# A 2x2 block product with seven products in the second matmul of a retention-plus-MLP kernel

## Chip, cores, metric

One core of a Trainium2 chip. The metric is device time in microseconds (us) of one execution. The kernel before takes 217.24 us (median of 4 runs, 216.81 to 218.08). Ratios and their intervals are those over fast runs, so they are not quite the ratio of the medians that are quoted. A run counts as slow when it is over 1.5% above the fastest of the same kernel in the same call.

## The reference

Causal linear attention with a decay per head, then an MLP with tanh-GELU. Four sequences of 768 tokens, 8 heads of 64, so 3072 tokens of width 512; the MLP is 512 to 2048 to 512.

```python
for t in range(S):
    state = gamma[None, :, None, None] * state + np.einsum('bhd,bhe->bhde', k[:, :, t], v[:, :, t])
    y[:, :, t] = scale * np.einsum('bhd,bhde->bhe', q[:, :, t], state)
# x: y as (3072, 512)
h = x @ w_in
g = 0.5 * h * (1.0 + np.tanh(c * (h + 0.044715 * h * h * h)))
out = g @ w_out
```

## The kernel before

The sequence is cut into 6 chunks of 128 positions; a chunk has 4 x 128 = 512 rows. "M1" of a chunk is `x @ w_in` with GELU, "M2" is `g @ w_out`. While TensorE works on M1 and M2 of chunk c, the attention of chunk n = c + 1 is woven in: GpSimd scales and casts its inputs (`prep`), VectorE transposes them (`att_T`) and evicts masked scores, that is, moves them from PSUM, where matmuls write, to SBUF (`att_AY`); TensorE does the small products.

```python
# GpSimd: scale q, transposed k, k; cast v   (once per chunk and sequence)
def prep(c, b):
    for nm in "qk":
        if c in BLK[nm]:
            prep_blk(nm, c, b)          # tensor_tensor, two SBUF inputs (fp32), fp16 out
    prep1(nc.gpsimd, "k", c, b)         # tensor_tensor, two SBUF inputs
    prep1(nc.gpsimd, "v", c, b)         # cast, one SBUF input
# pool of the scaled transposed k: bufs=2; freed by VectorE's transposes

# M2: 64 matmuls of 512 columns a chunk
def moe2_mm(ps, c, b, fcs, n0, n1):
    for fc in fcs:
        nc.tensor.matmul(out=ps[:, n0:n1],
            lhsT=g_sb[c, fc // 2][:, fc % 2, b * C:(b + 1) * C],
            rhs=w_out_sb[fc // (NF // NO)][:, fc % (NF // NO), n0:n1],
            start=(fc == 0), stop=(fc == NF - 1))

# the weaving, chunks 2 to 4; the key is the unit after which the work is issued:
# units 0 to 15 are M1 (0.86 us each), 16 to 31 are M2
after = {
    2: [(prep, n, 0)], 4: [(prep, n, 1)],
    6: [(prep, n, 2), (att_T, n, 0)], 8: [(prep, n, 3), (att_T, n, 1)],
    9: [(load, n + 1)] if n + 1 < NCk else [],
    12: [(att_AY, n, (), "att", n, (0, 1), None)],      # first scores
    13: [(att_T, n, 2)], 15: [(att_T, n, 3)],
    18: [(att_AY, n, (0, 1), "h", n, (2, 3), VE)],      # second scores
    # ... state sums after 20, 21, 27, 28
}
```

Of the kernel before, what the change touches and what calls it, by code (L numbers as in the profile page):

```python
# [9 lines left out]
F16 = mybir.dt.float16  # L10
F32 = mybir.dt.float32
AF = mybir.ActivationFunctionType
ALU = mybir.AluOpType
# [3 lines left out]
def kernel(  # L17
# [9 lines left out]
    nc = tc.nc  # L27
    B, H, S, Dh = q.shape
    C = 128
    NCk = S // C  # L30
    NHP = H // 2
    n_tok, d_model = out.shape
    d_ff = moe_w_in.shape[1]
    NF = d_ff // 128
# [23 lines left out]
    const = ctx.enter_context(tc.tile_pool(name="const", bufs=1))  # L58
    ld = ctx.enter_context(tc.tile_pool(name="ld", bufs=2 * B))
    pre = ctx.enter_context(tc.tile_pool(name="pre", bufs=2 * B))  # L60
    att = ctx.enter_context(tc.tile_pool(name="att", bufs=4))
    xp = ctx.enter_context(tc.tile_pool(name="xp", bufs=2))
    gp = ctx.enter_context(tc.tile_pool(name="gp", bufs=2))
    op = ctx.enter_context(tc.tile_pool(name="op", bufs=4))
    psum = ctx.enter_context(tc.tile_pool(name="psum", bufs=1, space=bass.MemoryType.PSUM))

    OQ, OK, OG, OT = 0, H, 2 * H, 2 * H + NHP
# [58 lines left out]
    def hold(nm, c, b, until):  # L126
# [19 lines left out]
        out=misc[:, 0:1], in_=zero[:, 0:1], func=AF.Gelu_apprx_tanh, scale=1.0  # L146
# [16 lines left out]
    for j in range(2):  # L163
        for hp in range(NHP):
            nc.vector.tensor_scalar(
                out=mask[:, j, hp],
                in0=cst[:, OT:OT + 128],
# [64 lines left out]
    def bank(tag, dt=F32, shape=(128, NHP, 128), name="ps"):  # L232
        return psum.tile(list(shape), dt, tag=tag, bufs=BANKS[tag], name=name)
# [156 lines left out]
    w_out_sb = [const.tile([128, NF // NO, d_model], F16, name=f"w_out{i}") for i in range(NO)]  # L390
# [16 lines left out]
    g_sb = {}  # L407

    def moe1_mm(c, fc, out, t0, t1):
        wi, wr = w_in_of[fc]  # L410
        for kc in range(NHP):
            nc.tensor.matmul(  # L412
                out=out,
                lhsT=w_in_sb[wi][:, kc, wr * 128:(wr + 1) * 128],
                rhs=xT[c][:, kc, t0:t1],
                start=(kc == 0),
                stop=(kc == NHP - 1),
                skip_group_check=True,
            )

    def g_tile(c, fc):
        if (c, fc // 2) not in g_sb:
            g_sb[c, fc // 2] = gp.tile([128, 2, B * C], F16, tag=f"g{fc // 2}", name="g")
        return g_sb[c, fc // 2]

    def gelu(out, in_):
        nc.scalar.activation(out=out, in_=in_, func=AF.Gelu_apprx_tanh, scale=1.0)  # L427

    def moe1(c, fc):
        h_ps = bank("h", shape=(128, B * C), name="h_ps")  # L430
        moe1_mm(c, fc, h_ps, 0, B * C)
        gelu(g_tile(c, fc)[:, fc % 2], h_ps)

    def moe1_two(c, fp, t0, t1):

        h_ps = bank("h", shape=(128, 2, B * C // 2), name="h_ps")
        for r in range(2):
            moe1_mm(c, 2 * fp + r, h_ps[:, r, 0:t1 - t0], t0, t1)
        gelu(g_tile(c, 2 * fp)[:, :, t0:t1], h_ps[:, :, 0:t1 - t0])

    o_ps = {}

    def moe2_mm(ps, c, b, fcs, n0, n1):
        for fc in fcs:
            nc.tensor.matmul(  # L445
                out=ps[:, n0:n1],
                lhsT=g_sb[c, fc // 2][:, fc % 2, b * C:(b + 1) * C],
                rhs=w_out_sb[fc // (NF // NO)][:, fc % (NF // NO), n0:n1],
                start=(fc == 0),
                stop=(fc == NF - 1),  # L450
            )

    def moe2(c, b, fcs, tag="o"):
        if fcs[0] == 0:
            o_ps[c, b] = bank(tag, shape=(128, d_model), name="o_ps")
        moe2_mm(o_ps[c, b], c, b, fcs, 0, d_model)

    def ev_O(c, b):
        ps = o_ps[c, b]
        rows = out[b * S + c * C:b * S + (c + 1) * C, :]  # L460
        o_sb = op.tile([128, d_model], F32, tag="o", name="o_sb")
        if b == B - 1 and c > 0:
            nc.vector.tensor_copy(out=o_sb, in_=ps)
        else:
            nc.scalar.copy(out=o_sb, in_=ps)  # L465
        if c == NCk - 1:
            eng = nc.scalar
        else:
            eng = nc.sync if c == 0 and b < B - 1 else nc.gpsimd
        eng.dma_start(out=rows, in_=o_sb)  # L470

    def moe2_last(c, b):

        hw = d_model // 2
        rows = out[b * S + c * C:b * S + (c + 1) * C, :]
        o_sb = op.tile([128, d_model], F32, tag="o", name="o_sb")
        for i in range(2):
            ps = bank("h", shape=(128, d_model), name="o_ps")
            m0, m1, m2 = i * hw, i * hw + hw // 2, (i + 1) * hw
            moe2_mm(ps, c, b, range(NF), m0, m2)  # L480
            if i == 0:
                nc.vector.tensor_copy(out=o_sb[:, m0:m2], in_=ps[:, m0:m2])  # L482
            else:
                nc.vector.tensor_copy(out=o_sb[:, m0:m1], in_=ps[:, m0:m1])
                nc.scalar.copy(out=o_sb[:, m1:m2], in_=ps[:, m1:m2])
            nc.sync.dma_start(out=rows[:, m0:m2], in_=o_sb[:, m0:m2])

    def run(units, after):
        for i, u in enumerate(units):
            u()  # L490
            for f, *args in after.get(i, ()):
                f(*args)

    VE, AC, PO, SY = nc.vector, nc.scalar, nc.gpsimd, nc.sync
# [88 lines left out]
    def units2(c, b, n=4, tag="o"):  # L583
        u = [(lambda i=i: moe2(c, b, range(i, i + n), tag)) for i in range(0, NF, n)]
        last = u[-1]
        u[-1] = lambda: (last(), ev_O(c, b))
        return u


    def preps(c, b):  # L590
# [15 lines left out]
    run(  # L606
        [u[i % 3][i // 3] for i in range(12)] + u[3],
        {
            8: [(preps, 1, 0)],
            10: [(att_T, 1, 0), (preps, 1, 1)],  # L610
            11: [(att_AY, 1, (), "att", 1, (0,), None)],
# [9 lines left out]
    for b in range(B):  # L621
# [5 lines left out]
            for fp in range(NF // 2)  # L627
        ],
        {
            1: [(att_AY, 1, (2,), "o", 1, (3,), VE)],  # L630
            3: [(att_S, 1, 2)],
            4: [(att_AY, 1, (3,), "o", 1, (), VE)],
            6: [(att_S, 1, 3)],
            8: [(att_T, 2, 0), (load, 3)],
            10: [(att_T, 2, 1)],
            12: [(att_AY, 1, (), "o", 2, (0, 1), None)],
            14: [(att_T, 2, 2)],
            15: [(att_T, 2, 3)],
        },
    )  # L640
    run(
        [x for b in range(B) for x in units2(1, b)],
        {
            2: [(att_AY, 2, (0, 1), "h", 2, (2, 3), AC)],
            4: [(att_S, 2, 0)],
# [5 lines left out]
    )  # L651


    for c in range(2, NCk - 1):
        n = c + 1
        after = {
            2: [(prep, n, 0)],
            4: [(prep, n, 1)],
            6: [(prep, n, 2), (att_T, n, 0)],
            8: [(prep, n, 3), (att_T, n, 1)],  # L660
            9: [(load, n + 1)] if n + 1 < NCk else [],
            12: [(att_AY, n, (), "att", n, (0, 1), None)],
            13: [(att_T, n, 2)],
            15: [(att_T, n, 3)],
            18: [(att_AY, n, (0, 1), "h", n, (2, 3), VE)],
            20: [(att_S, n, 0)],
            21: [(att_S, n, 1)],
            25: [(att_AY, n, (2, 3), "h", n, (), AC)],
            27: [(att_S, n, 2)],
            28: [(att_S, n, 3)],  # L670
        }
        run(
            [(lambda fc=fc: moe1(c, fc)) for fc in range(NF)]
            + [x for b in range(B) for x in units2(c, b)],
            after,
        )
    c = NCk - 1
    for fc in range(NF):
        moe1(c, fc)
    for b in range(B - 1):  # L680
        for x in units2(c, b):
            x()
    moe2_last(c, B - 1)


# [28 lines left out]
```

## Time and profile before

| | before |
|---|---|
| time | 217.24 us |
| TensorE busy | 207.2 us, 96% of the span |
| M2, a chunk | 64 matmuls of 512 columns, 13.8 us |
| GpSimd's preparations in M1 of a steady chunk | 16, back to back, 14.3 us |
| VectorE busy | 82.9 us, 38% |

TensorE bounds the kernel; the prediction shows the lines. The groups by shape (line, engine, operation, output from inputs, shapes, count, then busy us and mean ns of one, then idle time before) give what VectorE and GpSimd do over the whole run:

```profile
L278 DVE TENSOR_TENSOR a_sb<-a_ps,mask 128x512 f16<-128x512 f32 x48 | 30.2, 684 | 19.6 <-PE a_ps L265 19.5
L188 POOL TENSOR_TENSOR k<-k,cst 128x512 f16<-128x512 f32 x24 | 25.1, 1047 | 16.4 <-DMA k<-in_k_dram 16.4
...
L199 POOL TENSOR_TENSOR q<-q,cst 128x512 f16<-128x512 f32 x16 | 16.7, 1042 | 5.8 <-DMA q<-in_q_dram 5.8
```

GpSimd's products take two tensors from SBUF, 1.04 us each. VectorE's big group takes one from PSUM and one from SBUF.

### The profile page before, as it was taken

How to read it: one execution, taken by the hardware profiler on the slowest of the kernel's cores; microseconds unless marked ns; L12 is line 12 of the kernel's file. 1: busy time of each engine (PE TensorE's matmuls, PEld its weight loads, DVE VectorE, ACT ScalarE, POOL GpSimd, SP SyncE). 2: the span in 40 equal slices, each digit the busy share in tenths (PEclk: the TensorE clock that was granted, in tenths of full speed). 3: DMA queues.
4: the chain of work that ended last, by engine and by line, in shares of the span. 5: the costliest groups of instructions: out<-in, count | busy, mean ns of one | idle time of the engine just before them, and what ended most of it. 6: DMA issues, size and time to landing. Idle time of an engine off the chain costs nothing.

```text
span 215.8 us, 3912 instructions
## 1 busy us (share of the span) xinstructions
PE 207.2 (96%) x1544; PEld 112.9 (52%) x1544; DVE 82.9 (38%) x152; ACT 87.0 (40%) x150; POOL 96.9 (45%) x116
## 2 busy tenths in 40 slices
PE   7889999999979999999999999999999999999993
PEld 2447644457867655444545444545444545444462
DVE  3445200198635562153691343682344650100001
ACT  2585562254444233276223275223366123476120
POOL 3699200324169542699433799412399321100000
PEclk9999999999999999999999999999999999999999
DMA  7999999896899688998679977579910012100111
GB/s 172 288 249 207 206 205 240 201 319 129 176 242 190 107 156 160 267 266 125 104 140 241 264 140 117 80 153 252 260 37 3 0 49 87 62 0 0 52 75 71
DMA packets 124417, 32.88 MB, mean 152 GB/s; under 512 B 118064, under 2 KB 122544, under 8 KB 124400
## 3 DMA queue, kind: packets, MB, share of 16 engines
q1 hardware_dynamic: 107984, 20.58, 48.2%
q0 software_dynamic: 5584, 8.65, 17.0%
q10 hardware_dynamic: 10832, 3.41, 6.5%
q8 instruction: 12, 0.20, 0.4%
q14 instruction: 5, 0.04, 0.1%
HBM read 30.53 MB, written 6.29 MB: 171 GB/s over the span
## 4 chain that ended last, share of the span: by engine, by line
PE 83%; SPq 4%; DMA 4%; POOL 2%; ACT 2%; issue 1%; DVE 1%; ACTq 0%; POOLq 0%; DVEq 0%
PE o_ps L445 38%; PE h_ps L412 34%; SPq L114 4%; PE a_ps L265 3%; PE y_ps L300 3%; DMA iden<-rr_ident 2%; PE s_ps L319 2%; DMA q<-in_q_dram 2%; PE y_ps L287 2%; PE qkT_ps L242 1%; PE spin_ps L152 1%; POOL q L199 1%; POOL k L188 1%; ACT qkT L224 1%; ACT g L427 1%
## 5 line engine op out<-in xcount | busy, mean ns | idle before, releaser
L445 PE MATMUL o_ps<-w_out,g 128*128 128x512 f16 (+1 forms) x400 | 88.1, 371 | 0.0
L412 PE MATMUL h_ps<-xT,w_in 128*128 128x512 f16 (+2 forms) x488 | 86.6, 334 | 0.5 <-ACT g L427 0.5
L427 ACT ACTIVATE g<-h_ps 128x512 f16<-128x512 f32 (+1 forms) x98 | 57.4, 588 | 51.6 <-PE h_ps L412 51.6
L412 PEld LDWEIGHTS <-w_in 128*128 128x128 f16 x488 | 45.8, 98 | 36.9 <-issue 0.7
L445 PEld LDWEIGHTS <-g 128*128 128x128 f16 x400 | 37.7, 98 | 38.8
L278 DVE TENSOR_TENSOR a_sb<-a_ps,mask 128x512 f16<-128x512 f32 x48 | 30.2, 684 | 19.6 <-PE a_ps L265 19.5
L188 POOL TENSOR_TENSOR k<-k,cst 128x512 f16<-128x512 f32 x24 | 25.1, 1047 | 16.4 <-DMA k<-in_k_dram 16.4
L470 POOL DMA_DIRECT2D out_dram<-o_sb x17 | 9.7, 568 | 46.4 <-ACT o_sb L465 36.8
L465 ACT COPY o_sb<-o_ps 128x512 f32<-128x512 f32 x19 | 11.0, 585 | 42.3 <-PE o_ps L445 37.1
L345 POOL TENSOR_TENSOR stg<-st,cst 128x512 f32<-128x512 f16 x16 | 16.4, 1045 | 10.2 <-DVE st L336 9.1
L336 DVE TENSOR_TENSOR st<-s_ps,stg 64x256 f16<-64x256 f32 x32 | 13.5, 421 | 17.8 <-PE s_ps L319 17.2
L199 POOL TENSOR_TENSOR q<-q,cst 128x512 f16<-128x512 f32 x16 | 16.7, 1042 | 5.8 <-DMA q<-in_q_dram 5.8
L251 DVE STREAM_TRANSPOSE qkT<-q 128x512 f16<-128x512 f16 x16 | 11.2, 700 | 13.1 <-POOL q L199 13.1
L224 ACT CAST xT<-y_ps 128x512 f16<-128x512 f32 x15 | 8.3, 588 | 12.2 <-PE y_ps L300 12.1
L199 POOL TENSOR_TENSOR kT<-kT,cst 128x512 f16<-128x512 f32 x12 | 12.5, 1042 | 0.0
L188 DVE TENSOR_TENSOR q<-q,cst 128x512 f16<-128x512 f32 x7 | 4.8, 686 | 19.0 <-DMA q<-in_q_dram 18.9
L152 PE MATMUL spin_ps<-zero 128*128 128x512 f16 x32 | 9.9, 449 | 1.2 <-DVE zero L144 1.2
L482 DVE COPY o_sb<-o_ps 128x256 f32<-128x256 f32 x1 | 0.4, 424 | 25.2 <-PE o_ps L445 25.2
L185 POOL CAST v<-v 128x512 f16<-128x512 f32 x16 | 9.6, 601 | 0.0
L183 ACT CAST v<-v 128x512 f16<-128x512 f32 x8 | 5.0, 622 | 11.1 <-issue 7.9
L251 DVE STREAM_TRANSPOSE qkT<-kT 128x512 f16<-128x512 f16 x12 | 8.3, 690 | 1.7 <-POOL kT L199 1.7
L226 DVE CAST xT<-y_ps 128x512 f16<-128x512 f32 x9 | 5.9, 687 | 7.8 <-PE y_ps L300 7.8
(33 smaller groups left out, 96.9 us busy)
## 6 DMA issues: line engine op xcount, KB each, us to landing
k<-in_k_dram SPq DMA_DIRECT2D x22, 256.0 KB, 4.4
v<-in_v_dram SPq DMA_DIRECT2D x18, 256.0 KB, 4.4
out_dram<-o_sb POOLq DMA_DIRECT2D x17, 256.0 KB, 3.5
q<-in_q_dram SPq DMA_DIRECT2D x64, 64.0 KB, 2.6
kT<-in_k_dram SPq DMA_DIRECT2D x48, 64.0 KB, 2.7
w_in<-in_moe_w_in_dram POOLq DMA_DIRECT2D x4, 512.0 KB, 9.6
w_out<-in_moe_w_out_dram POOLq DMA_DIRECT2D x4, 512.0 KB, 15.0
v<-in_v_dram ACTq DMA_DIRECT2D x6, 256.0 KB, 5.5
```

Source lines behind the costliest of these rows:

```text
L152: nc.tensor.matmul(out=ps, lhsT=zero[:, 0:128], rhs=zero, start=True, stop=True)
L188: eng.tensor_tensor(out=t, in0=src, in1=cst[:, col:col + H].unsqueeze(2).broadcast_to([128, H, Dh]), op=ALU.mult,)
L199: nc.gpsimd.tensor_tensor(out=t, in0=ld_all((key, c))[:, b * NHP:(b + 1) * NHP].rearrange("p hp a d -> p (hp a) d"), in1=cst[:, col:col + ...
L224: eng.copy(out=out, in_=in_)
L251: nc.vector.transpose(out=t[:, i].rearrange("p hp t -> p (hp t)"), in_=blk16.pop((nm, c, b)).rearrange("p ha d -> p (ha d)"),)
L278: nc.vector.tensor_tensor(out=s, in0=ps[j], in1=mask[:, j], op=ALU.mult)
L336: eng.tensor_tensor(out=st[sl, :, b, sl], in0=s_ps[sl, :, sl], in1=stg[sl, :, b, sl], op=ALU.add,)
L345: nc.gpsimd.tensor_tensor(out=stg[:, :, b], in0=st[:, :, b], in1=cst[:, OG:OG + NHP].unsqueeze(2).broadcast_to([128, NHP, 128]), op=ALU.mult,)
L412: nc.tensor.matmul(out=out, lhsT=w_in_sb[wi][:, kc, wr * 128:(wr + 1) * 128], rhs=xT[c][:, kc, t0:t1], start=(kc == 0), stop=(kc == NHP - ...
L427: nc.scalar.activation(out=out, in_=in_, func=AF.Gelu_apprx_tanh, scale=1.0)
L445: nc.tensor.matmul(out=ps[:, n0:n1], lhsT=g_sb[c, fc // 2][:, fc % 2, b * C:(b + 1) * C], rhs=w_out_sb[fc // (NF // NO)][:, fc % (NF // NO ...
L465: nc.scalar.copy(out=o_sb, in_=ps)
```

## The change

The intent: M2 of a chunk is a 2x2 block product (rows in halves by sequence parity, the inner dimension in halves by parity of the 128-blocks, columns in halves). The block form with seven products needs 7/8 of the matmul columns. Price: four sums of 512 elements for every four GELU blocks, 16 a chunk (VectorE, fp16, both inputs in SBUF), 16 sums of weight blocks once, and PSUM banks that ScalarE copies out in the middle of an accumulation ("snapshots"). Its core:

```diff
+    def g_sums(c, i, p0=0, p1=2):
+        ...
+        tt(t[1], q[0, 1], q[1, 1], ALU.add)          # tt: nc.vector.tensor_tensor
+        tt(t[3], q[0, 0], q[0, 1], ALU.subtract)
+        tt(t[2], t[1], q[0, 0], ALU.subtract)
+        tt(t[4], q[1, 0], t[2], ALU.subtract)
+    PROD = (                      # bank, left, right, opens, closes
+        ("X", (0, 0), (0, 0), True, False),
+        ("Z", 1, 1, True, False),
+        ("X", 2, 2, False, False),
+        ("Z", 4, (1, 1), False, True),
+        ("X", 3, 3, False, False),
+        ("Z", (1, 0), (1, 0), True, True),
+        ("X", (1, 1), 4, False, True),
+    )
+    # units_w(c): 7 products x 2 row halves x 8 matmuls of 256 columns; after products
+    # 0, 1, 2 ScalarE copies the bank out, after 3, 4, 5 VectorE adds such a copy
@@ chunks 2 to 5
+        for i in range(4):
+            at = 4 * i + 3
+            after[at] = [(g_sums, c, i)] + after.get(at, [])
+        run([(lambda fc=fc: moe1(c, fc)) for fc in range(NF)] + units_w(c), after)
```

(Cut: chunk 1, where the sums come in halves; the stores; pools of `x`, `g` and `o` go to one buffer.)

More of the change, by code (lines that the diff above doesn't have):

```diff
@@ L61 @@
     att = ctx.enter_context(tc.tile_pool(name="att", bufs=4))
-    xp = ctx.enter_context(tc.tile_pool(name="xp", bufs=2))
-    gp = ctx.enter_context(tc.tile_pool(name="gp", bufs=2))
-    op = ctx.enter_context(tc.tile_pool(name="op", bufs=4))
+    xp = ctx.enter_context(tc.tile_pool(name="xp", bufs=1))
+    gp = ctx.enter_context(tc.tile_pool(name="gp", bufs=1))
+    op = ctx.enter_context(tc.tile_pool(name="op", bufs=1))
     psum = ctx.enter_context(tc.tile_pool(name="psum", bufs=1, space=bass.MemoryType.PSUM))
@@ L421, in g_tile @@
     def g_tile(c, fc):
-        if (c, fc // 2) not in g_sb:
-            g_sb[c, fc // 2] = gp.tile([128, 2, B * C], F16, tag=f"g{fc // 2}", name="g")
-        return g_sb[c, fc // 2]
+        if (c, fc // 4) not in g_sb:
+            g_sb[c, fc // 4] = gp.tile([128, 4, B * C], F16, tag=f"g{fc // 4}", name="g")
+        r = fc % 4 // 2 * 2
+        return g_sb[c, fc // 4][:, r:r + 2]
     def gelu(out, in_):
@@ L446, in moe2_mm @@
                 out=ps[:, n0:n1],
-                lhsT=g_sb[c, fc // 2][:, fc % 2, b * C:(b + 1) * C],
+                lhsT=g_sb[c, fc // 4][:, fc % 4, b * C:(b + 1) * C],
                 rhs=w_out_sb[fc // (NF // NO)][:, fc % (NF // NO), n0:n1],
@@ L456, in moe2 @@
         moe2_mm(o_ps[c, b], c, b, fcs, 0, d_model)
+    o_0 = {}
     def ev_O(c, b):
@@ L460, in ev_O @@
         rows = out[b * S + c * C:b * S + (c + 1) * C, :]
-        o_sb = op.tile([128, d_model], F32, tag="o", name="o_sb")
-        if b == B - 1 and c > 0:
-            nc.vector.tensor_copy(out=o_sb, in_=ps)
-        else:
-            nc.scalar.copy(out=o_sb, in_=ps)
-        if c == NCk - 1:
-            eng = nc.scalar
-        else:
-            eng = nc.sync if c == 0 and b < B - 1 else nc.gpsimd
-        eng.dma_start(out=rows, in_=o_sb)
-    def moe2_last(c, b):
-        hw = d_model // 2
-        rows = out[b * S + c * C:b * S + (c + 1) * C, :]
-        o_sb = op.tile([128, d_model], F32, tag="o", name="o_sb")
-        for i in range(2):
-            ps = bank("h", shape=(128, d_model), name="o_ps")
-            m0, m1, m2 = i * hw, i * hw + hw // 2, (i + 1) * hw
-            moe2_mm(ps, c, b, range(NF), m0, m2)
-            if i == 0:
-                nc.vector.tensor_copy(out=o_sb[:, m0:m2], in_=ps[:, m0:m2])
-            else:
-                nc.vector.tensor_copy(out=o_sb[:, m0:m1], in_=ps[:, m0:m1])
-                nc.scalar.copy(out=o_sb[:, m1:m2], in_=ps[:, m1:m2])
-            nc.sync.dma_start(out=rows[:, m0:m2], in_=o_sb[:, m0:m2])
+        if b % 2 not in o_0:
+            o_0[b % 2] = op.tile([128, 2, d_model], F32, tag=f"o{b % 2}", name="o_sb")
@@ new lines, in ev_O, with w_q, tt @@
+        o_sb = o_0[b % 2][:, b // 2]
+        nc.scalar.copy(out=o_sb, in_=ps)
+        eng = nc.sync if b < B - 1 else nc.gpsimd
+        eng.dma_start(out=rows, in_=o_sb)
+    hw = d_model // 2
+    NP = NF // 2
+    t_w = {i: const.tile([128, NP, hw], F16, name=f"t_w{i}") for i in (1, 2, 3, 4)}
+    s_g = {i: const.tile([128, NP, 2, C], F16, name=f"s_g{i}") for i in (1, 2, 3, 4)}
+    def w_q(i, r, x):
+        return w_out_sb[i].rearrange("p (f r) (x n) -> p r x f n", r=2, x=2)[:, r, x]
+    def tt(out, in0, in1, op):
+        nc.vector.tensor_tensor(out=out, in0=in0, in1=in1, op=op)
@@ new lines, in w_sums @@
+    def w_sums(i):
+        t = {j: t_w[j][:, 2 * i:2 * i + 2] for j in t_w}
+        tt(t[1], w_q(i, 0, 1), w_q(i, 0, 0), ALU.subtract)
+        tt(t[3], w_q(i, 1, 1), w_q(i, 0, 1), ALU.subtract)
+        tt(t[2], w_q(i, 1, 1), t[1], ALU.subtract)
+        tt(t[4], w_q(i, 1, 0), t[2], ALU.subtract)
+    def g_sums(c, i, p0=0, p1=2):
+        g = g_sb[c, i].rearrange("p (f r) (a b t) -> p r b f a t", r=2, a=2, b=2)
+        q = {(r, b): g[:, r, b][:, :, p0:p1] for r in range(2) for b in range(2)}
+        t = {j: s_g[j][:, 2 * i:2 * i + 2, p0:p1] for j in s_g}
+        tt(t[1], q[0, 1], q[1, 1], ALU.add)
+        tt(t[3], q[0, 0], q[0, 1], ALU.subtract)
+        tt(t[2], t[1], q[0, 0], ALU.subtract)
+        tt(t[4], q[1, 0], t[2], ALU.subtract)
@@ new lines, in lhs, with rhs @@
+    def lhs(c, key, fp, a):
+        if key in s_g:
+            return s_g[key][:, fp, a]
+        r, b = key
+        b = 2 * a + b
+        return g_sb[c, fp // 2][:, 2 * (fp % 2) + r, b * C:(b + 1) * C]
+    def rhs(key, fp):
+        if key in t_w:
+            return t_w[key][:, fp]
+        r, x = key
+        return w_out_sb[fp // 2][:, 2 * (fp % 2) + r, x * hw:(x + 1) * hw]
+    PROD = (
[7 more added lines that the diff above has]
+    )
@@ new lines, in units_w, with bank_of, mm, o_tile @@
+    def units_w(c):
+        ps, o_sb, snap = {}, {}, {}
+        last = c == NCk - 1
+        def bank_of(k, a, new):
+            if new:
+                if last:
+                    ps[k, a] = bank(("o", "h")[a], shape=(128, 2, hw), name="o_ps")[:, 0]
+                else:
+                    if a == 0:
+                        ps[k] = bank("o", shape=(128, 2, hw), name="o_ps")
+                    ps[k, a] = ps[k][:, a]
+            return ps[k, a]
+        def mm(n, a):
+            k, lk, rk, new, stop = PROD[n]
+            po = bank_of(k, a, new)
+            for fp in range(NP):
+                nc.tensor.matmul(
+                    out=po,
+                    lhsT=lhs(c, lk, fp, a),
+                    rhs=rhs(rk, fp),
+                    start=(new and fp == 0 and (last or a == 0)),
+                    stop=(stop and fp == NP - 1),
+                    skip_group_check=True,
+                )
+        def o_tile(b):
+            if b not in o_sb:
+                o_sb[b] = op.tile([128, 2, d_model], F32, tag=f"o{b}", name="o_sb")
+            return o_sb[b]
+        def snap_tile(nm):
+            if nm not in snap:
+                snap[nm] = op.tile([128, 2, hw], F32, tag=nm, name=nm)
+            return snap[nm]
+        def ev(n, a0, a1):
+            k = PROD[n][0]
+            p = ps[k, a0].unsqueeze(1) if last else ps[k]
+            if n in (0, 1, 2):
+                nc.scalar.copy(out=snap_tile(f"s{n}")[:, a0:a1], in_=p)
+            elif n in (3, 4, 5):
+                b, x = {3: (0, 1), 4: (1, 1), 5: (0, 0)}[n]
+                tt(
+                    o_tile(b)[:, a0:a1, x * hw:(x + 1) * hw],
+                    p,
+                    snap[f"s{5 - n if n > 3 else 2}"][:, a0:a1],
+                    ALU.add,
+                )
+            else:
+                nc.scalar.copy(out=o_tile(1)[:, a0:a1, 0:hw], in_=p)
+        def store(b, a0, a1, n0, n1, eng):
+            rows = out.rearrange("(a b t) n -> b t a n", a=2, b=2)
+            eng.dma_start(
+                out=rows[b, c * C:(c + 1) * C, a0:a1, n0:n1], in_=o_sb[b][:, a0:a1, n0:n1]
+            )
+        def unit(n, a):
+            mm(n, a)
+            if not last:
+                if a == 1:
+                    ev(n, 0, 2)
+                    if n > 4:
+                        store(n - 5, 0, 2, 0, d_model, nc.gpsimd)
+            elif n < 6:
+                ev(n, a, a + 1)
+                if n == 5:
+                    store(0, a, a + 1, 0, d_model, nc.scalar)
+                if n == 4 and a == 1:
+                    store(1, 1, 2, hw, d_model, nc.sync)
+            elif a == 0:
+                ev(n, a, a + 1)
+                store(1, 0, 1, 0, d_model, nc.scalar)
+            else:
+                t, p = o_tile(1)[:, 1], ps["X", 1]
+                nc.vector.tensor_copy(out=t[:, 0:hw // 2], in_=p[:, 0:hw // 2])
+                nc.scalar.copy(out=t[:, hw // 2:hw], in_=p[:, hw // 2:hw])
+                store(1, 1, 2, 0, hw, nc.sync)
+        return [(lambda n=n, a=a: unit(n, a)) for n in range(7) for a in range(2)]
@@ L608 @@
         {
+            3: [(w_sums, 0)],
+            6: [(w_sums, 1)],
             8: [(preps, 1, 0)],
@@ L629 @@
         {
-            1: [(att_AY, 1, (2,), "o", 1, (3,), VE)],
-            3: [(att_S, 1, 2)],
-            4: [(att_AY, 1, (3,), "o", 1, (), VE)],
-            6: [(att_S, 1, 3)],
+            1: [(att_AY, 1, (2,), "o", 1, (3,), VE), (w_sums, 2)],
+            2: [(w_sums, 3)],
+            3: [(att_S, 1, 2), (g_sums, 1, 0, 0, 1)],
+            4: [(att_AY, 1, (3,), "o", 1, (), VE), (g_sums, 1, 1, 0, 1)],
+            6: [(att_S, 1, 3), (g_sums, 1, 2, 0, 1)],
+            7: [(g_sums, 1, 3, 0, 1)],
             8: [(att_T, 2, 0), (load, 3)],
+            9: [(g_sums, 1, 0, 1, 2)],
             10: [(att_T, 2, 1)],
+            11: [(g_sums, 1, 1, 1, 2)],
             12: [(att_AY, 1, (), "o", 2, (0, 1), None)],
+            13: [(g_sums, 1, 2, 1, 2)],
             14: [(att_T, 2, 2)],
-            15: [(att_T, 2, 3)],
+            15: [(g_sums, 1, 3, 1, 2), (att_T, 2, 3)],
         },
@@ L641 @@
     run(
-        [x for b in range(B) for x in units2(1, b)],
+        units_w(1),
         {
@@ L651 @@
     )
-    for c in range(2, NCk - 1):
+    for c in range(2, NCk):
         n = c + 1
-        after = {
+        after = {} if n == NCk else {
             2: [(prep, n, 0)],
@@ L667 @@
             21: [(att_S, n, 1)],
-            25: [(att_AY, n, (2, 3), "h", n, (), AC)],
-            27: [(att_S, n, 2)],
-            28: [(att_S, n, 3)],
-        }
-        run(
-            [(lambda fc=fc: moe1(c, fc)) for fc in range(NF)]
-            + [x for b in range(B) for x in units2(c, b)],
-            after,
-        )
-    c = NCk - 1
-    for fc in range(NF):
-        moe1(c, fc)
-    for b in range(B - 1):
-        for x in units2(c, b):
-            x()
-    moe2_last(c, B - 1)
+            24: [(att_AY, n, (2, 3), "h", n, (), AC)],
+            26: [(att_S, n, 2)],
+            27: [(att_S, n, 3)],
+        }
+        for i in range(4):
+            at = 4 * i + 3
+            after[at] = [(g_sums, c, i)] + after.get(at, [])
+        run([(lambda fc=fc: moe1(c, fc)) for fc in range(NF)] + units_w(c), after)
 _INS = ['q', 'k', 'v', 'moe_w_in', 'moe_w_out']
```

## The prediction

> **What bounds the kernel now.** I read the page's busy shares first, then the chain of work that ended last, then the groups by shape, then the timelines of VectorE and GpSimd over one steady chunk.
>
> ```profile
> PE 207.2 (96%) x1544; PEld 112.9 (52%) x1544; DVE 82.9 (38%) x152; ACT 87.0 (40%) x150; POOL 96.9 (45%) x116
> ...
> PE 83%; SPq 4%; DMA 4%; POOL 2%; ACT 2%; issue 1%; DVE 1%; ACTq 0%; POOLq 0%; DVEq 0%
> ```
>
> TensorE is busy 96% of the span and carries 83% of the chain: it is the bound, and VectorE, ScalarE and GpSimd each have over half their time free on average. From 71 us on the chain is TensorE alone, so there a matmul saved is time saved, and any wait put in front of TensorE is time lost. The chain in order of time gives the price of a matmul by width, and the places of one steady chunk (chunk 3, which starts at 121.19):
>
> ```profile
> 16.98 0.87 PE h_ps L412 x8
> ...
> 121.19 11.22 PE h_ps L412 x52
> 132.41 0.55 PE a_ps L265 x16
> 132.97 2.70 PE h_ps L412 x12
> 135.66 2.59 PE o_ps L445 x12
> 138.25 0.45 PE y_ps L287 x8
> 138.70 0.55 PE a_ps L265 x16
> ...
> 143.13 3.45 PE o_ps L445 x16
> ```
>
> The reader is to see three things. Eight 256-column matmuls take 0.87 us (109 ns each), sixteen 512-column ones 3.45 us (216 ns each): half the width is almost exactly half the time. The M1 of a chunk (16 groups of 4, each 0.863 us) is interrupted by the scores of the next chunk's heads 11.22 us after its start. And the second scores come at 138.70, 17.5 us after the start: both need transposes from VectorE.
>
> **What the Trainium skill says.** (1) "TensorE: Matmul & The Clock Gate", section Back-to-back issue gap: N / 2.4 + 2.5 ns, so 109.2 ns for 256 columns and 215.8 for 512; the trace agrees (109, 216). (2) "VectorE: DVE Perf Modes", the perf-mode tier table: a tensor_tensor of 16-bit SBUF operands runs at two elements a cycle and never at four; the errata section has (N + 151) / 0.96 ns, N the cycles. At one element a cycle 512 gives 691 ns and the trace's masked score evictions take 684. The kernel before has no 16-bit two-input sum; for 512 elements at two a cycle I estimate from the page (256 + 151) / 0.96 = 424 ns. (3) "SBUF — State Buffer", Who interferes with whom: a VectorE instruction with two SBUF inputs contends with a GpSimd instruction that reads SBUF, and the one that comes second blocks fully. The trace holds one clear case:
>
> ```profile
> 7.45 0.69 DVE L188 TENSOR_TENSOR q<-q,cst 128x512 f16<-128x512 f32 x1 [2.83 <-DMA q<-in_q_dram]
> ...
> 7.81 1.23 POOL L188 TENSOR_TENSOR k<-k,cst 128x512 f16<-128x512 f32 x1 [1.26 <-DMA k<-in_k_dram]
> ```
>
> The GpSimd product normally takes 1.04 us; started inside a two-input VectorE product it took 1.23, about the time that the other still had to stream. The reverse case, VectorE held by GpSimd, does not occur in this trace, because VectorE's other work reads PSUM or one SBUF operand. (4) "PSUM — Partial Sum Buffer", the four PSUM rules: the flag that opens a group clears the bits of the whole bank, and a synchronised read of a partial sum is allowed. The change sets it once per bank for non-last chunks and reads by semaphore. No run shows this yet.
>
> **The change part by part.** *TensorE.* M2 of one chunk is 64 matmuls of 512 columns, 64 x 0.2157 = 13.80 us. It becomes 7 products x 2 row halves x 8 = 112 matmuls of 256 columns, 112 x 0.1088 = 12.18 us. Saved: 1.62 us a chunk, 8.1 us over five. That is the most that can be won: 217.2 - 8.1 = 209.1, or 3.7%.
>
> *ScalarE and the banks.* Four 512-column copies a chunk instead of three, 0.58 us each. The products alternate between two banks, so a snapshot has the 16 matmuls of the other bank, 1.74 us, before TensorE returns; in M2 ScalarE has no GELU. Hidden. VectorE's three PSUM-plus-snapshot sums (about 0.69 each, against one copy) have the same 1.74 us and are hidden if VectorE is not behind.
>
> *Weight sums.* 16 sums once, half in M2 of chunk 0, where VectorE idles, half in chunk 1's M1 just ahead of evictions that M1's second half needs (about 3 us in a busy queue).
>
> *Activation sums.* 16 a chunk in M1, in four groups after GELUs 3, 7, 11 and 15, each put ahead of the next chunk's transposes in VectorE's queue. One group: three starts 0.33 apart and one that waits for its predecessor, about 1.5 us. VectorE's queue in chunk 3, from M1's start, nothing else in its way (a GELU ends 0.64 us after its matmuls; a pair of transposes occupies 1.2 us, four score evictions 2.4): sums 0 at 4.1 to 5.6, transposes 0 to 6.8; sums 1 wait for GELU 7 at 7.5, to 9.0, transposes 1 to 10.2; sums 2 wait for GELU 11 at 11.0, to 12.5; score evictions to 14.9; transposes 2 to 16.1; sums 3 to 17.6; transposes 3 to 18.9. TensorE reaches the first scores at 11.2 (transposes 1 done at 10.2: no wait). It starts M2 at 14.4, the second product at 16.15, whose last pair needs the first sum of group 3 at about 16.8 (there at 16.5: just in time). The scores of head 3 are wanted at 17.7, but its transposes end at 18.9: **a wait of 1.2 us**. So even without port conflicts chunks 2, 3 and 4 give back 3 x 1.2 = 3.6 us. In chunk 1 the same kind of ledger (8 weight sums, then 32 half-size sums, between the state sums and the transposes) puts the first scores and the fourth transposes about 2 us late in all. Chunk 5 has no attention beside it and keeps its 1.6. Sum: 217.2 - 8.1 + 3.6 + 2 = 214.7.
>
> *Port.* GpSimd is not idle during those sums:
>
> ```profile
> 122.82 1.06 POOL L199 TENSOR_TENSOR q<-q,cst 128x512 f16<-128x512 f32 x1
> 123.82 1.05 POOL L199 TENSOR_TENSOR kT<-kT,cst 128x512 f16<-128x512 f32 x1
> 124.83 1.04 POOL L188 TENSOR_TENSOR k<-k,cst 128x512 f16<-128x512 f32 x1
> 125.81 0.60 POOL L185 CAST v<-v 128x512 f16<-128x512 f32 x1
> ```
>
> Four such rounds run without a gap from 122.82 to 137.11, 14.3 us, over nearly all of M1. Twelve of the sixteen sums meet them. If GpSimd merely gives up the port for each sum (about 0.3 us of streaming), its fourth kT comes 12 x 0.3 = 3.6 us later, at 18.0 instead of 14.4 after the start, and VectorE loses perhaps 0.5 us at each group: transposes 3 end near 20.3, a wait of 2.6 us a chunk. Over three chunks that is 7.8 instead of 3.6, and chunk 1 some 3 to 4 instead of 2: about 220.
>
> **The rivals.** *A, strict alternation.* Every sum waits for the GpSimd product in flight and then GpSimd takes its turn: a group of four costs some 5 us instead of 1.5. My ledger then has transposes 1 at 15.5 (TensorE waits 4.3 us at the first scores), the first sum of group 3 at 23.6 and transposes 3 near 26: 8 us lost a chunk, 25 over three, and 5 to 12 in chunk 1, where GpSimd prepares chunk 2 meanwhile. The time would be 235 to 246. For it: the page's wording and the 1.23 us; against it: the trace has no VectorE instruction that waited for GpSimd. *B, all of it hidden.* The sums cost less than estimated or slip into gaps, the scores wait under 0.3 us: 209 to 212. For it: VectorE is 38% busy; against it: in M1 the queue adds up to 13.2 us of work that cannot start before 4.1, and has waits for GELUs in it. *C, PSUM turnaround.* TensorE waits for snapshots between accumulations. Four bank hand-overs of about 0.7 us against 1.74 us of cover speak against it; only behind a late VectorE would it appear, under 1 us a chunk.
>
> **Range and chances.** The no-conflict ledger gives 214.7, the mild conflict 220, alternation 235 to 246, full hiding 210. I give them about 30, 30, 25 and 15 in a hundred. The middle of that is about 219. The range that leaves a tenth on each side runs from 211 to 242. Under 212.8 is faster by over 2%: 0.22. Over 221.5 is slower: 0.38. Between: 0.40.
>
> **What would show it.** TensorE's M2 group should be 560 matmuls of 256 columns for chunks 1 to 5 at a spacing of 109 ns; if their stretches are not 1.6 us shorter per chunk, the first step is wrong. The mean of the 16-bit sums tells the port step: near 0.42 us and GpSimd's products at 1.04, there is no conflict; sums near 0.42 and products above 1.2, the mild one; sums near 1 us, alternation. In the waits, TensorE's scores (or their weight loads) should wait for VectorE's transposes by 1 to 3 us in each of chunks 2 to 4. If no such wait appears and the time is under 212, the ledger of VectorE's queue was wrong; if TensorE waits at snapshots instead, C was.

## The result

The changed kernel takes 249.03 us (247.56 to 250.35, 4 runs) against 217.24: ratio 1.143, interval 1.136 to 1.151. It is 14% slower, and outside the predicted range. The page after (busy us of each engine; the granted clock by slice; the chain by engine and by line, which is the work that ended last, followed back at each step to what it had waited for):

```profile
span 248.5 us, 4458 instructions
...
PE 212.8 (86%) x1768; PEld 139.5 (56%) x1768; DVE 161.5 (65%) x277; ACT 90.4 (36%) x158; POOL 98.6 (40%) x108
...
PEclk9999999999965999995979999788999869999999
...
PE 57%; DVE 36%; DMA 2%; ACT 2%; issue 1%; POOL 0%; ACTq 0%
DVE s_g L481 23%; PE o_ps L544 23%; PE h_ps L412 18%; DVE qkT L251 6%; PE o_ps L446 6%; DVE a_sb L278 3%; PE y_ps L300 3%; DMA k<-in_k_dram 2%; PE a_ps L265 2%; PE s_ps L319 2%; PE qkT_ps L242 2%; ACT g L428 1%; PE spin_ps L152 1%; PE y_ps L287 1%; DVE t_w L481 1%
```

VectorE went from 1% of the chain to 36%, and the activation sums alone hold 23%, about 58 us, although there are only 96 of them. Their groups by shape, the 512-element ones:

```profile
L481 DVE TENSOR_TENSOR s_g<-g 128x512 f16<-128x512 f16 x32 | 32.1, 1044 | 24.8 <-ACT g L428 24.8
...
L481 DVE TENSOR_TENSOR s_g<-s_g,g 128x512 f16<-128x512 f16 x16 | 13.2, 822 | 0.0
...
L481 DVE TENSOR_TENSOR s_g<-g,s_g 128x512 f16<-128x512 f16 x16 | 8.5, 533 | 0.6
```

1.04, 0.82 and 0.53 us in the mean, for what I had at 0.42. The means hide the distribution. Here is chunk 3 (its M1 starts at 138.41), VectorE first, then GpSimd in the same stretch (start, duration, engine, line, operation; in brackets idle time before and its cause):

```profile
142.74 6.03 DVE L481 TENSOR_TENSOR s_g<-g 128x512 f16<-128x512 f16 x1 [4.63 <-ACT g L428]
...
149.03 0.41 DVE L481 TENSOR_TENSOR s_g<-s_g,g 128x512 f16<-128x512 f16 x1
149.48 0.42 DVE L481 TENSOR_TENSOR s_g<-g,s_g 128x512 f16<-128x512 f16 x1
149.82 0.70 DVE L251 STREAM_TRANSPOSE qkT<-q 128x512 f16<-128x512 f16 x1
...
152.54 1.26 DVE L481 TENSOR_TENSOR s_g<-s_g,g 128x512 f16<-128x512 f16 x1
```

```profile
142.32 1.04 POOL L188 TENSOR_TENSOR k<-k,cst 128x512 f16<-128x512 f32 x1
143.31 0.60 POOL L185 CAST v<-v 128x512 f16<-128x512 f32 x1
143.88 1.04 POOL L199 TENSOR_TENSOR q<-q,cst 128x512 f16<-128x512 f32 x1
...
147.45 1.04 POOL L199 TENSOR_TENSOR q<-q,cst 128x512 f16<-128x512 f32 x1
151.20 1.14 POOL L199 TENSOR_TENSOR kT<-kT,cst 128x512 f16<-128x512 f32 x1 [2.71 <-DVE qkT L251]
152.30 1.22 POOL L188 TENSOR_TENSOR k<-k,cst 128x512 f16<-128x512 f32 x1
```

One sum, issued while GpSimd ran back to back, took 6.03 us (6.01 in chunk 4). GpSimd's products in that time kept their 1.04 us: it gave nothing. The sum ended at 148.8, right after GpSimd's run stopped at 148.5. And GpSimd stopped only because its next product needed a tile that VectorE's transposes, queued behind the sum, had to free. From 151.2 on the two alternate: sums of up to 1.27 us, products of 1.14 to 1.22. In the chain of the changed kernel, where this M1 starts at 138.58, the same stretch reads (start, us, what):

```profile
138.58 3.51 PE h_ps L412 x16
142.11 0.61 ACT g L428
142.74 6.72 DVE s_g L481 x3
...
165.58 0.04 issue
165.62 0.61 PE a_ps L265 x8
```

From 142.1 to 165.6 TensorE is not on the chain: the last part of the second scores starts 27.0 us after M1's start, where the kernel before started them at 17.5. The time of each chunk, from the first matmul of its M1 to that of the next chunk (for chunk 5 to its last matmul), read from TensorE's timeline in each trace; the rows from e1 on are experiments told below:

| chunk | 1 | 2 | 3 | 4 | 5 |
|---|---|---|---|---|---|
| before | 37.1 | 32.1 | 32.1 | 31.1 | 27.8 |
| the change | 45.7 | 41.2 | 41.3 | 38.8 | 26.4 |
| e1, no sums | 35.5 | 30.7 | 30.7 | 29.6 | 26.4 |
| e2b, GpSimd only writes | 37.2 | 32.3 | 32.3 | 31.3 | 26.4 |
| e7, preparations and transposes early | 46.4 | 30.6 | 30.6 | 29.6 | 26.4 |
| e10, dummy matmuls in the wait | 46.4 | 39.7 | 42.3 | 38.8 | 26.4 |
| e11, block product in 4 and 5 only | 36.5 | 32.3 | 32.3 | 29.6 | 26.4 |

Chunk 5 has no attention beside it, so GpSimd is quiet, and there the change gains 1.5 us, nearly what was predicted.

### The profile page after: what moved, and what is told of

It is laid out like the page before. It is cut to its first block, busy times and chain, and to the rows that moved or that the text cites. A ratio compares the mean times of both kernels' runs of the same rounds, so it can differ in the third digit from the quotient of the medians.

```text
span 248.5 us, 4458 instructions
## 1 busy us (share of the span) xinstructions
PE 212.8 (86%) x1768; PEld 139.5 (56%) x1768; DVE 161.5 (65%) x277; ACT 90.4 (36%) x158; POOL 98.6 (40%) x108
## 4 chain that ended last, share of the span: by engine, by line
PE 57%; DVE 36%; DMA 2%; ACT 2%; issue 1%; POOL 0%; ACTq 0%
DVE s_g L481 23%; PE o_ps L544 23%; PE h_ps L412 18%; DVE qkT L251 6%; PE o_ps L446 6%; DVE a_sb L278 3%; PE y_ps L300 3%; DMA k<-in_k_dram 2%; PE a_ps L265 2%; PE s_ps L319 2%; PE qkT_ps L242 2%; ACT g L428 1%; PE spin_ps L152 1%; PE y_ps L287 1%; DVE t_w L481 1%
## 5 line engine op out<-in xcount | busy, mean ns | idle before, releaser
L481 DVE TENSOR_TENSOR s_g<-g 128x512 f16<-128x512 f16 (+1 forms) x48 | 39.9, 871 | 25.9 <-ACT g L428 25.8
L544 PEld LDWEIGHTS <-s_g 128*128 128x128 f16 x320 | 31.3, 101 | 6.7 <-DVE s_g L481 1.5
L265 PE MATMUL a_ps<-qkT 64*128 64x128 f16 x192 | 10.6, 240 | 26.7 <-DVE qkT L251 19.0
L544 PE MATMUL o_ps<-t_w,s_g 128*128 128x256 f16 x240 | 32.2, 285 | 1.0 <-DVE s_g L481 1.0
L188 POOL TENSOR_TENSOR k<-k,cst 128x512 f16<-128x512 f32 x24 | 26.4, 1100 | 16.1 <-DMA k<-in_k_dram 16.1
L544 PEld LDWEIGHTS <-g 128*128 128x128 f16 x240 | 23.4, 99 | 3.8 <-issue 0.6
L481 DVE TENSOR_TENSOR o_sb<-o_ps,s 128x512 f32<-128x512 f32 (+1 forms) x18 | 10.9, 603 | 19.7 <-PE o_ps L544 15.7
L567 ACT COPY s<-o_ps 128x512 f32<-128x512 f32 (+1 forms) x18 | 9.3, 516 | 29.5 <-PE o_ps L544 28.3
L544 PE MATMUL o_ps<-w_out,g 128*128 128x256 f16 x160 | 19.8, 274 | 0.0
L481 DVE TENSOR_TENSOR s_g<-s_g,g 128x512 f16<-128x512 f16 (+1 forms) x24 | 17.5, 731 | 0.0
L446 PE MATMUL o_ps<-w_out,g 128*128 128x512 f16 x64 | 14.8, 379 | 0.0
```

Of the source, the lines that this page charges most:

```text
L188: eng.tensor_tensor(out=t, in0=src, in1=cst[:, col:col + H].unsqueeze(2).broadcast_to([128, H, Dh]), op=ALU.mult,)
L265: nc.tensor.matmul(out=ps[j][:, hp], lhsT=t[j * 64:(j + 1) * 64, 1, hp], rhs=t[j * 64:(j + 1) * 64, 0, hp], start=True, stop=True,)
L446: nc.tensor.matmul(out=ps[:, n0:n1], lhsT=g_sb[c, fc // 4][:, fc % 4, b * C:(b + 1) * C], rhs=w_out_sb[fc // (NF // NO)][:, fc % (NF // NO ...
L481: nc.vector.tensor_tensor(out=out, in0=in0, in1=in1, op=op)
L544: nc.tensor.matmul(out=po, lhsT=lhs(c, lk, fp, a), rhs=rhs(rk, fp), start=(new and fp == 0 and (last or a == 0)), stop=(stop and fp == NP ...
```

## The experiments

Theories: **P**, the sums wait for GpSimd's reads of SBUF (the prediction's port step; a trace shows who waits for whom, not the port); **Q**, VectorE's queue in M1 is simply too long; **T**, TensorE waits for snapshots between accumulations. Diffs are against the changed kernel unless said otherwise. A single look has one run, so its state is unknown; effects of over 5% are read from its time, smaller ones from rounds or from single instructions and chunks in its trace. Medians are of all runs: two of e6's four, one of e7's four and one of e9's six are slow.

| run | us | right result |
|---|---|---|
| the change | 249.0 | yes |
| e1 no sums | 210.2 (one run) | no |
| e2 GpSimd only writes | 238.4 (one run) | no |
| e2b the same, loads paced | 216.6 (one run) | no |
| e3 one-input work in place of the sums | 238.2 (one run) | no |
| e4 four tiles for scaled keys | 254.1 (one run) | yes |
| e5 write-only gaps on GpSimd | 250.4 (one run) | yes |
| e6 preparations early | 234.8, ratio to before 1.083 | yes |
| e7 and transposes early | 220.6, ratio 1.012 | yes |
| e8 and chunk 1 plain | 221.2, ratio 1.017 | yes |
| e9 block product from chunk 3 on | 218.3, ratio 1.000 | yes |
| e10 dummy matmuls in the wait | 251.2, ratio 1.154 | yes |
| e11 block product in chunks 4 and 5 | 214.9, ratio 0.985 | yes |

### e1: no sums

```diff
     def g_sums(c, i, p0=0, p1=2):
+        return
...
         if key in s_g:
-            return s_g[key][:, fp, a]
+            key = {1: (0, 1), 2: (1, 1), 3: (0, 0), 4: (1, 0)}[key]
```

> The activation sums are left out and the products that used them read the GELU tiles instead (wrong result on purpose); matmuls, banks, snapshots and stores stay. Theory P (GpSimd and VectorE share a port, the sums wait for GpSimd's products) and theory Q (VectorE's queue in M1 is simply too long) both expect 209 to 211 us: the 8.1 us of TensorE come out whole and nothing waits. Theory T (TensorE waits for the snapshots between accumulations) expects 215 us or more, with waits of the products on ScalarE.

Measured: 210.18 us against 217.38, every chunk 1.5 us shorter than before (in the exact figures, 1.46 to 1.52), clock 1.000. TensorE's part of the change, the banks, the snapshots and the stores cost nothing that shows, nor do the pools that went to one buffer, which e1 keeps. T falls: no wait of a product of M2 on ScalarE appears in the waits. All of the loss comes with the sums.

### e2 and e2b: GpSimd writes but does not read

```diff
-            eng.tensor_tensor(out=t, in0=src, in1=cst[...], op=ALU.mult)
+            for _ in range(2):                      # e2 (cast: once)
+                nc.gpsimd.memset(t, 0.0)
+            nc.gpsimd.tensor_copy(out=t[0:1, 0, 0:1], in_=src[0:1, 0, 0:1])   # e2b only
```

> GpSimd's preparations of chunks 2 to 5 become plain zero fills of the same tiles, about as long (two per product, one per cast), which read nothing (wrong result on purpose); the sums stay as they are. P expects every sum near its 0.42 us (no 6 us one), waits of the scores for the transposes near the 1 us a chunk that the blind ledger had, and 211 to 217 us. Q expects the sums to cost as much as before and 240 us or more.

Measured: 238.39 us, which by the number alone speaks for neither. But its last matmul ended at 211.6 us; the rest was loads that no instruction waited for any more and that trickled in after the work was done. The experiment had a fault of its own, so it was repeated with one element read of each load.

> As e2_preps_write_only, whose last loads had lost their readers and ended 24 us after the last matmul; here GpSimd still reads one element of each loaded tile, so that the loads keep their pace (wrong result on purpose). P expects every activation sum of chunks 2 to 4 under 0.5 us, chunks 2, 3 and 4 at about 32, 32 and 31 us as in e2, and now a time of 214 to 219 us. Q expects 240 us or more.

Measured: 216.58 us. GpSimd is no less busy than in the change (104.6 us against 98.6), but its preparations hardly read. The sums by shape in e2b:

```profile
L483 DVE TENSOR_TENSOR s_g<-g 128x512 f16<-128x512 f16 x32 | 12.0, 417 | 29.1 <-ACT g L430 29.1
L483 DVE TENSOR_TENSOR s_g<-g,s_g 128x512 f16<-128x512 f16 x16 | 6.8, 425 | 0.5
L483 DVE TENSOR_TENSOR s_g<-s_g,g 128x512 f16<-128x512 f16 x16 | 6.7, 418 | 0.0
```

Each of these 64 sums lasts 0.38 to 0.43 us. With the same sums in the same queue the loss is gone: P holds, Q falls as the main cause. Q keeps a small part: chunks 1 to 4 are 1.6 to 1.7 us longer in e2b than in e1.

### e3: VectorE busier, but with one SBUF input

```diff
+        if c >= 2:      # four transposes of 512 elements, same tiles, same order; flat: s_g's tiles
+            for o, s in ((flat[1], g_sb[c, i][:, 3]), (flat[3], g_sb[c, i][:, 2]),
+                         (flat[2], flat[1]), (flat[4], flat[2])):
+                nc.vector.transpose(out=o, in_=s)
+            return
```

> In chunks 2 to 5 the four sums of a group become four transposes of 512 elements, one SBUF input each, written to the same tiles with the same waits (wrong result on purpose). VectorE then has more work than with the sums (0.6 us a start instead of 0.33), and GpSimd is as busy as ever. P expects no instruction of VectorE over 0.75 us in chunks 2 to 4, GpSimd's products back at 1.04 us, a wait of some 3 us a chunk from the longer queue, and 225 to 232 us (chunk 1 keeps its real sums and its loss of about 8.7). Q expects 249 us or more, as the queue is longer.

Measured: 238.17 us, a miss above the range, but in the direction of P. Chunks 2, 3 and 4 take 35.7, 36.1 and 36.5 us, against 41.2, 41.3 and 38.8 with the sums, although each of the 64 replacements lasts 0.67 to 0.71 us. The halved clock after the long waits remains, and it was not in the expected figure. No VectorE instruction of chunks 2 to 4 is over 0.75 us, as P said. GpSimd's kT products are back at 1043 ns. More work on VectorE that needs one SBUF input costs less than less work that needs two.

### e4: let GpSimd run without a stop

```diff
-        t = pre.tile([128, NHP * 4, 32], F16, tag=tag, bufs=6 if nm == "q" else 2, name=tag)
+        t = pre.tile([128, NHP * 4, 32], F16, tag=tag, bufs=6 if nm == "q" else 4, name=tag)
```

> Only the pool of GpSimd's scaled key blocks grows from 2 to 4 tiles, so that GpSimd no longer has to stop in mid chunk for VectorE's transposes. If a sum that finds GpSimd running back to back gets no turn until GpSimd stops (starvation), the first sum of chunks 3 and 4 now waits about 12 us instead of 6, until all sixteen preparations are done, and the time is 252 to 260 us. If the two take turns (alternation), the first sums are no longer than 1.5 us and the time is at or below that of the change, 240 to 249 us.

Measured: 254.1 us, 2% above the change in a single run; in its trace chunks 3 and 4 are 2.0 and 2.3 us longer (43.3 and 41.1). More buffers made it slower. VectorE's and GpSimd's timelines of chunk 3 in e4:

```profile
142.17 12.51 DVE L481 TENSOR_TENSOR s_g<-g 128x512 f16<-128x512 f16 x2 [4.62 <-ACT g L428]
154.60 0.41 DVE L481 TENSOR_TENSOR s_g<-s_g,g 128x512 f16<-128x512 f16 x1
```

```profile
152.48 1.03 POOL L188 TENSOR_TENSOR k<-k,cst 128x512 f16<-128x512 f32 x1
153.46 0.60 POOL L185 CAST v<-v 128x512 f16<-128x512 f32 x1
```

The first sum waited until the last of the sixteen preparations ended at 154.06, and lasted 12.18 us; two sums together took 12.51 us. Starvation, not alternation, sets the first group. In chunk 4 it is 12.48 us again. In chunk 2 of e4 the sums did get a turn now and then (three of 3.7 to 3.8 us).

### e5: gaps that do not read

```diff
         h16[nm, c, b] = t
+        if c >= 2:
+            nc.gpsimd.memset(gapt, 0.0)     # 64 elements, after every preparation
```

> After each preparation of GpSimd in chunks 2 to 5 comes a zero fill of 64 elements, which reads nothing (some 0.15 us, 14 to 16 a chunk). If a waiting sum gets the port whenever GpSimd has an instruction between two products that does not read, the 6 us first sums shrink to some 1.5 us, a group of four takes about 5 us, and the time is 238 to 247 us. If only a stop of GpSimd lets it in, the first sums are at least as long as in the change (6 us and more) and the time is 248 to 255 us.

Measured: 250.36 us, and the first two sums of chunk 3 took 7.04 us together (6.37 in the change). A write-only instruction of 0.14 us between two reads does not let VectorE in. A wait of GpSimd does.

### e10: is the halved clock a loss of its own?

The granted clock fell to half for several stretches after the long waits (0.93 in the mean).

```diff
-            12: [(att_AY, n, (), "att", n, (0, 1), None)],
+            12: [(spin, 24), (att_AY, n, (), "att", n, (0, 1), None)],
```

> The change, with 24 dummy matmuls (5.2 us at full clock) before the first scores in chunks 2 to 4, in the time that TensorE waits for VectorE's transposes anyway; the result stays right. If the waits themselves are the whole loss, the time stays at 248 to 251 us. If a part of the loss is the halved clock after each wait (in the change's trace some 2 us of each of these chunks), the mean clock rises from 0.93 and the time falls to 241 to 246 us.

Measured: 251.21 us with the mean clock of the profiled run at 0.966. The clock rose, the time did not fall. That total hides two opposite changes. Up to the second scores the chain runs through VectorE, and a slow TensorE costs nothing there; after them it is TensorE's. In the change 16 matmuls there took 3.05 us in chunk 2 and 2.75 in chunk 3, against 1.8 in chunk 4. The chain of the change in chunk 2, then that of e10 in chunks 2 and 3:

```profile
125.65 3.05 PE o_ps L544 x16
```

```profile
126.71 1.85 PE o_ps L544 x16
...
167.19 3.53 PE o_ps L544 x16
```

In chunk 2 the dummies kept the clock up to this place, and the chunk is 1.5 us shorter than in the change (39.7 against 41.2). In chunk 3 the clock fell again between the first scores and the second, and stayed low for longer: 1.0 us more. Chunk 4, where the change was at full clock here already, is unchanged, and chunk 1, which has no dummies, came out 0.7 us longer. So the halved clock, itself a consequence of the waits, is a further cost: 1.5 us in chunk 2, shown by e10, and about as much in chunk 3, read from the chain.

### e6 and e7: move GpSimd's reads and VectorE's transposes

```diff
-            2: [(prep, n, 0)],
-            4: [(prep, n, 1)],
-            6: [(prep, n, 2), (att_T, n, 0)],
-            8: [(prep, n, 3), (att_T, n, 1)],
+            6: [(att_T, n, 0)],                                   # e6
+            8: [(att_T, n, 1)],
+            16: [(prep, n + 1, b) for b in range(B)] if n + 1 < NCk else [],
# e7 in addition: all four att_T of chunk n after units 0 and 1
# both: four tiles for scaled keys; chunk 3's preparations at the head of M2 of chunk 1
```

> The preparations of the chunk after next go to M2, where VectorE has no two-input sum, and the scaled key blocks get 4 tiles; the result stays right. P expects the sums of chunks 2 to 4 near 0.42 us, the blind ledger's wait of 1 to 2 us a chunk left, chunk 1 still about 8 us slow, in all 221 to 228 us. Q (VectorE's queue as such) expects no gain over the change, 245 us or more, since VectorE's work and its order are unchanged.

Measured: 234.78 us (231.49 and 233.73 in the two fast runs), ratio 1.083 (1.07 by the two fast runs): 14 to 16 us better than the change, but a miss. Its chain still holds sums of chunks 2 and 3 stretched by GpSimd, and GpSimd waited for loads, 14.9 us for two, and 9.3 us for a transpose: a part of the preparations still ran into the next M1.

> As e6_preps_early, and the next chunk's transposes are issued at the head of M1, while VectorE waits for the first GELUs. P with the ledger expects the 1 to 2 us waits of chunks 2 to 4 to go too and each of them to gain the 1.6 us: 217 to 223 us, what is left being chunk 1. If the transposes wait for late preparations instead, no better than e6.

Measured: 220.60 us, ratio 1.012. From chunk 2 on the chain of e7 is TensorE's matmuls, without a VectorE piece in the long ones:

```profile
129.39 11.35 PE h_ps L412 x52
141.29 2.70 PE h_ps L412 x12
143.99 2.62 PE o_ps L544 x24
...
159.99 11.35 PE h_ps L412 x52
```

Chunks 2 to 4 take 30.6, 30.6 and 29.6 us, 1.5 less than before each: the full gain. The whole deficit sits in chunk 1, 46.4 us instead of 37.1, where GpSimd prepares chunk 2 beside the sums.

### e8 and e9: where the early preparations run out of data

e8 is e7 with M2 of chunk 1 as in the kernel before; e9 also leaves chunk 2 as it was.

```diff
-        units_w(1),                                             # e8, e9; and no g_sums of chunk 1
+        [x for b in range(B) for x in units2(1, b)],
# e9 in addition: chunk 2 with units2, and prep and att_T of chunk 3 where they were before
```

> As e7_T_early, with M2 of chunk 1 as in the kernel before (eight products; no sums beside the preparations of chunk 2). P with the ledger expects four chunks that gain 1.6 us each and no loss: 210 to 214 us, ratio to before 0.97 to 0.985, faster than both kernels. If chunk 1's loss in the change does not come from its sums, 217 us or more.

Measured: 221.24 us, ratio 1.017. A miss: chunk 1 fell from e7's 46.4 us to 36.0, but chunk 2 rose from 30.6 to 40.7. GpSimd's timeline of e8 says why:

```profile
87.29 1.05 POOL L199 TENSOR_TENSOR kT<-kT,cst 128x512 f16<-128x512 f32 x1 [8.70 <-DMA v<-in_v_dram]
88.86 1.04 POOL L188 TENSOR_TENSOR k<-k,cst 128x512 f16<-128x512 f32 x1 [0.52 <-DMA k<-in_k_dram]
```

The preparations of chunk 3, meant for M2 of chunk 1, waited for their loads and ended at 101, 13 us into M1 of chunk 2. In e7 they ended at 100, but there the slow chunk 1 had put M1 of chunk 2 off to 98.6. On the page before, the DMA engines are 90% busy or more in 9 of the first 16 slices (up to 86 us), which leaves little room to load earlier.

> The block product only where its sums meet no preparation: M2 of chunks 1 and 2 as in the kernel before, chunks 3, 4 and 5 with seven products, their neighbours' preparations in the M2 before and the transposes at the head of M1, as in e7_T_early, where each such chunk gained 1.5 us. P expects 217.3 - 3 x 1.5 = 212.8, range 211.5 to 214.5 us, ratio 0.973 to 0.987. If the early preparations come late again, as in e8_c1_plain, 216 us or more.

Measured: 218.30 us, ratio 1.000, interval 0.996 to 1.004. A miss for the same reason: the preparations of chunk 4 waited 8.16 us for a key block and ended at 130, where M1 of chunk 3 needed the transposes. Chunks 4 and 5 gained 1.5 us each, and chunk 3 lost 5.2.

### e11: only where GpSimd can be quiet

The block product in chunks 4 and 5 alone. Chunk 5's query and key blocks are scaled in M2 of chunk 3, its values cast in M2 of chunk 4; its untransposed keys, which nothing reads (there is no state after the last chunk), are neither loaded nor scaled. The scaled keys have four tiles, as in e6.

```diff
+        plain = c < 4                     # chunks 1 to 3: units2 and the old schedule
+            16: [(prep_qk, 5, b) for b in range(B)] if c == 3 else [],
+        # chunk 4: att_T of chunk 5 after units 0 and 1
+            16: [(prep1, nc.gpsimd, "v", n, b) for b in range(B)],
```

> The block product in chunks 4 and 5 alone, where GpSimd can be made quiet during M1: chunk 5's query and key blocks are scaled in M2 of chunk 3, its values cast in M2 of chunk 4, its untransposed keys (which nothing reads) are neither loaded nor scaled; chunks 1 to 3 as in the kernel before. P expects every sum near 0.42 us and 1.5 us gained in each of two chunks: 217.5 - 3 = 214.5, range 213 to 216.5 us, ratio 0.98 to 0.995. If the blocks of chunk 5 still land too late for M2 of chunk 3, 217 us or more.

Measured: 214.88 us (213.96 to 215.36, 6 runs) against 218.28, ratio 0.985, interval 0.982 to 0.988. Sums by shape in e11:

```profile
L481 DVE TENSOR_TENSOR s_g<-g 128x512 f16<-128x512 f16 x16 | 6.4, 440 | 15.6 <-ACT g L428 15.5
```

Of its 32 sums 31 are at 0.41 to 0.43 us and one at 0.72. Chunks 4 and 5 gain 1.5 us each. This is the fastest kernel here with the right result, 1.5% under the kernel before: clear of the noise, but small. It also drops chunk 5's unused key work, whose share was not measured apart; the same chunk times, 29.6 and 26.4, stand in e7, which keeps that work. Chunks 1 to 3 moved by -0.5, +0.1 and +0.1 us.

## Why the prediction was wrong

- **TensorE's saving**: said 8.1 us. Right, a little large: e1 shows 1.5 us in each of the five chunks, 7.4 us in the span (215.8 to 208.4).
- **Snapshots and banks hidden (rival C under 1 us)**: right, by e1.
- **A sum without conflict takes 0.42 us**: right, 417 to 425 ns in e2b.
- **The queue's wait**: said 1.2 us in each of chunks 2 to 4 and 2 in chunk 1, total 214.7. Right in kind, near in size: e2b less e1 is 1.6 or 1.7 us in each of the four chunks, 6.6 in all where 5.6 was said, and the time is 216.6.
- **The port**: this step failed. Its sentence was "If GpSimd merely gives up the port for each sum (about 0.3 us of streaming)", and it got as much weight as the case without conflict, and more than alternation. GpSimd did not give it up: in chunks 3 and 4 the first sum waited 6 us, until GpSimd stopped by itself, and everything behind it on VectorE waited too. The change less e2b is 8.5, 8.9, 9.0 and 7.5 us in chunks 1 to 4, 33.9 us. Some 5 us of this are the halved clock that the waits brought, which the prediction did not have: 1.5 in chunk 2 (e10), and by the chain about as much in chunk 3 and 1.7 in chunk 1, where 16 matmuls of M1 took 3.53 us instead of 1.8. Together: -7.4 + 6.6 + 33.9 = +33.1; the spans differ by 248.5 - 215.8 = 32.7.
- **Rival A** named the conflict, but with turns, and had 235 to 246 (its parts, -8.1, 25 and 5 to 12, add to 239 to 246). Its ledger put transposes 1 at 15.5, the first sum of group 3 at 23.6 and transposes 3 near 26 us after M1's start; chunk 3 shows 17.2, 24.7 and 27.0. That is near by luck. It let a sum in after one product and gave every group some 5 us; the first three groups of chunk 3 took 7.2, 3.4 and 3.4. The first sum waited through six more products and casts (6.03 us), and through thirteen in e4. The halved clock came on top.
- **The sign for the port step**, a mean of the sums, could not tell these apart: 1.04 us reads as "alternation", and is three sums of 3.8 to 6.0 us among many of 0.4 to 1.3.
- **The evidence I held back from**: I noted that the trace before had no VectorE instruction that waited for GpSimd, and took that as an argument against. It only meant that the case had not come up. The case that I had, 1.23 us, was read too well: GpSimd lost 0.19 us while the VectorE product ran on for 0.33. None of the seven two-input VectorE products in that trace was started inside a GpSimd one.

What stays open: what decides when a waiting sum gets its turn. In chunk 1 the two took turns from the first sum that met a preparation on; in chunk 2 a sum came in only before some casts; in chunks 3 and 4 the first one never did until GpSimd stopped. e5 excludes that a write-only instruction of 0.14 us in between is enough. No run here tells more.

## What to carry to other kernels

Before giving VectorE an operation with two SBUF inputs, look at what GpSimd does at that time, not at VectorE's busy share: a sum of 0.42 us waited up to 12 us behind GpSimd's stream of reads, and everything queued on VectorE waited with it. Place such work where GpSimd does not read, or move GpSimd's reads; check first that their data has landed by then. And if GpSimd's run ends only because it waits for VectorE, more buffers can make things worse.

## What the Trainium skill lacked or had wrong

- "SBUF — State Buffer", Who interferes with whom, is right that a VectorE instruction with two SBUF inputs contends with a GpSimd instruction that reads SBUF and not with one that only writes: the first two sums of a group last 1.04 us in the mean in the change, 0.42 beside fills (e2b). It lacks that the one that waits can be passed over by a whole run of instructions: 6.03 us in the change, about 12 in e4, not one instruction's 1.04.
- The same section does not say whether a short write-only instruction between two reads gives a waiting VectorE instruction its turn. Here it did not (e5, two sums in 7.04 us).
- "TensorE: Matmul & The Clock Gate", section Back-to-back issue gap, gives about 131 ns a matmul as the sustained rate for 512 columns; this kernel's steady stream runs at 216 ns, which is the page's other formula.
